# Attention beside an MLP on one core: the scale of Q from sums in PSUM, lengths once a chunk, V's read-outs first

## The chip, the cores and the metric

The kernel runs on one core of a Trainium2 chip. Its engines work side by side, each through its own instructions in order: TensorE (PE in the profile; PEld are its weight loads), VectorE (DVE), ScalarE (ACT), GpSimd (POOL) and SyncE (SP), which here only issues DMAs. The metric is the device time of one execution in microseconds; the three runs of the kernel before took 1353.08, 1352.74 and 1349.31 us, median 1352.74.

## What is computed

One input x of 2048 rows and 640 columns is normalized. The result is x plus an attention block of 32 heads (head size 20) plus an MLP block of width 1536, both on the normalized rows:

```python
def _A_ref(x, wqkv, wo):
    qkv = (x @ wqkv).reshape(B, S, 3, H, Dh).transpose(2, 0, 3, 1, 4)
    q, k, v = qkv[0], qkv[1], qkv[2]
    p = softmax(einsum("bhqd,bhkd->bhqk", q, k) * Dh ** -0.5)
    o = einsum("bhqk,bhkd->bhqd", p, v)
    return o.transpose(0, 2, 1, 3).reshape(B, S, D) @ wo
def _B_ref(x, w1, b1, w2, b2):
    y = layernorm(x)
    return gelu(y @ w1 + b1) @ w2 + b2
xn = layernorm(A_x)
return A_x + _A_ref(xn, A_wqkv, A_wo) + _B_ref(xn, B_w1, B_b1, B_w2, B_b2)
```

S = 2048, D = 640, H = 32, everything float32.

## The kernel before, in words

The kernel has a **head** (to about 218 us of the span), which makes Q, K and V and prepares the weights, and a long **loop** over head pairs, half sequences and key blocks, into which the MLP and the output projection are woven by credits. The change lies in the head alone, and the head's order is the order in which the program is written: each engine gets its instructions in that order and takes them strictly one after the other.

Float32 values are split into a high and a low float16 part, and a product is made of three float16 passes (`PASS`). So that the parts lie in range, each weight matrix gets a scale, a power of two from the sum of its squares. `squares` adds up along the free dimension on ACT (one accumulator column for each piece), `pow2` adds over partitions with a matmul against a 128x128 tile of ones (`L111`), adds the columns on DVE (`L112`) and makes a power of two from the exponent bits (`L113` to `L117`, `exponents` at `L99`); `scale_of` makes from it the scale (`L421`) and, for Q and K, the factor `qks` for the way back (`L424`), which the read-outs of Q and K use. `split_qkv` (`L429` on ACT, `L430` on DVE) makes the parts.

**The start.** The first 512 rows are normalized, transposed on PE (`L535`, against the identity `ident`; the fifth column block follows at `L539` into the one buffer of the PSUM pool `psM`, tag `m`), while ACT sums the squares of Q's weights. Behind the sixteen transposes of the first four blocks PE runs the sum for the scale of Q, then the copies `xnt` (`L543`, `L544`) and splits alternate with the first products.

**The chunks.** The rows go in four chunks `c` of 512. For each, five tile pairs `tt` (256 columns of Q or K) are made: `qk` (`L323`), its read-out `qk_out` (`L338` on ACT, `L339` on DVE, two stores to `qkscr` from SP), and the squares of what was read out, `qk_sq`, into a tile `sq` (even `tt`: pool `pa`, two buffers; odd `tt`: the tag `qs` of the pool `stp`, also two). `lengths` takes squares from the list `pend` and adds them head by head with small matmuls (`L368`, four for each block of 128 columns) in PSUM; it is called with four blocks at `tt == 3` and with the remaining six behind V's second tile (in the last chunk behind V's first). Then four tiles of V follow: `vproj` (`L396`) and `vproj_out` (`L406` on ACT; for half of the key blocks `L408` on DVE too).

**Other work between.** `some(n)` takes the next `n` steps of the weight work (`weights`): squares of w2 and w1, their scales, `factors`, which at `tt == 4` of chunk 1 squares b1 (`L95`) and sums it by `pow2` on PE, and the splits (`L126` to `L128`), among which the scale of wo is made in chunk 2. `norm_a`, `norm_b` and `norm_c` normalize the next chunk's rows; `norm_c` ends with a DMA from POOL that stores 512 row scales of 4 bytes each (`rscr`, `L272`). Chunk 1 is transposed on PE (`transp`, `transp_out`). Chunks 2 and 3 are transposed by DMA: `turn` writes a `row` tile (`L304` on ACT, `L305` on DVE; three buffers) and SP issues its transposition (`L306`). It is called behind `qk_out` for row 0 at `tt == 2`, rows 1 and 2 at `tt == 3`, row 3 at `tt == 4`; when row 3 has landed, SP stores the chunk (`L309`) for the MLP.

**Buffers.** A tile takes the buffer of its tag that came free first, and its first writer waits until the last user of that buffer has finished; for a `row` tile that is the DMA. The pool `psS` has three PSUM buffers, taken in turn by the products, V's tiles, the transposes and the sums of `pow2` other than Q's and K's.

Of the kernel before, what the change touches and what calls it, by code (L numbers as in the profile page):

```python
# [16 lines left out]
P = 128  # L17
# [25 lines left out]
def mha_mlp_kernel(tc, x, wqkv, wo, w1, b1, w2, b2, out):  # L43
# [4 lines left out]
    with (  # L48
# [53 lines left out]
        def pow2(acc, tag):  # L102

            lo = keep.tile([P, 1], F32, name=f"lo_{tag}")
            hi = keep.tile([P, 1], F32, name=f"hi_{tag}")
            if tag in ("q", "k"):
                pt = psM.tile([P, 512], F32, tag="m", name="mxp")
            else:
                pt = psS.tile([P, 2, 512], F32, tag="s", name="mxp")[:, 0, :]
            n = acc.shape[1]  # L110
            nc.tensor.matmul(pt[:, :n], ones, acc, start=True, stop=True)  # L111
            nc.vector.tensor_reduce(lo, pt[:, :n], AX.X, ALU.add)  # L112
            nc.vector.tensor_scalar(lo, lo, 2.0**-100, 2.0**120, ALU.max, ALU.min)  # L113

            nc.vector.tensor_scalar(lo.bitcast(I32), lo.bitcast(I32), 0x7F000000, 1,
                                    ALU.bitwise_and, ALU.logical_shift_right)
            nc.vector.tensor_scalar(lo, lo, 2.0**64, None, ALU.mult)  # L117
            exponents(lo, hi)
            return lo, hi

        pw = {}
# [40 lines left out]
        with tc.tile_pool(name="pa", bufs=2) as pa, tc.tile_pool(name="pa1", bufs=1) as pa1, tc.manual_schedule():  # L162
# [135 lines left out]
            def turn(c, j):  # L298

                if j == 0:  # L300
                    xnts[c] = pa.tile([P, KD, 2, 512], F16, tag="xnt", name=f"xnt{c}")
                xv = xts[c][j].rearrange("p (k n) -> p k n", k=KD)
                row = pa.tile([P, KD, 2, P], F16, tag="row", name="row", bufs=3)
                nc.scalar.activation(row[:, :, 0, :], xv, AF.Copy)  # L304
                nc.vector.tensor_sub(row[:, :, 1, :], xv, row[:, :, 0, :])  # L305
                nc.sync.dma_start(xnts[c].rearrange("p k s t -> p (k s) t")[:, :, j * P : (j + 1) * P],  # L306
                                  row.rearrange("p k s n -> p (k s n)"), transpose=True)
# [105 lines left out]
            accs, scales = {}, {}  # L413
# [4 lines left out]
            def scale_of(tag):  # L418
                pw[tag] = pow2(accs[tag], tag)
                scales[tag] = keep.tile([P, 1], F32, name=f"s_{tag}")  # L420
                nc.vector.tensor_scalar(scales[tag], pw[tag][1], 4096.0, None, ALU.mult)  # L421
                if tag in "qk":
                    q = "qk".index(tag)
                    nc.vector.tensor_scalar(qks[:, q : q + 1], pw[tag][0], QKTOP, 2.0**-22, ALU.min, ALU.mult)  # L424
# [107 lines left out]
            pt = [pts[0][:, 0], pts[0][:, 1], pts[1][:, 0], pts[1][:, 1]]  # L532
            for j in range(4):
                for k in range(KD - 1):
                    nc.tensor.transpose(pt[k][:, j * P : (j + 1) * P], xts[0][j][:, k * P : (k + 1) * P], ident)  # L535
            scale_of("q")
# [5 lines left out]
            for k in range(KD):  # L542
                nc.scalar.activation(xnts[0][:, k, 0, :], pt[k], AF.Copy)  # L543
# [6 lines left out]
            for c in range(4):  # L550
                nxt = c + 1 if c < 3 else None
                for tt in range(5):
# [11 lines left out]
                    if tt == 3:  # L564
                        lengths(4)
# [37 lines left out]
                for j in range(4):  # L603
                    ps = vproj(c, j)
                    if j == (0 if c == 3 else 1):
                        lengths(10)
                    if c == 0:
# [13 lines left out]
                    vproj_out(c, j, ps)  # L621
# [658 lines left out]
```

## Time and profile before

| | |
|---|---|
| runs | 1353.08, 1352.74, 1349.31 us; median 1352.74 |
| the profiled execution | 1349.61 us, of it span 1347.7 us; mean granted clock 0.999 |
| busy over the span | PE 1330.8 us (99%), ACT 1128.6 (84%), DVE 1055.8 (78%), POOL 37.9 (3%) |
| the head | to 218.51 us, where the loop's first matmul (`L709`) stands |
| HBM traffic | 82.14 MB read, 42.51 MB written |

How to read the lines that follow. A **timeline** row is: start in us, duration in us, engine, line of the kernel, operation, output<-inputs, shapes, count; in brackets the idle time of the engine before it and what ended it. Neighbouring instructions of one kind are merged into one row ("x4"), with the first start and the stretch to the last end. A **stage table** row is: the stretch, its length, then busy time and count of instructions for PE, PEld, DVE, ACT and POOL, then the granted PE clock (1.00 is full), the DMA share and GB/s. A **DMA issue** row gives the median time from issue to landing at its end. Matmuls are pipelined: the duration of one is longer than the distance to the next.

### The profile page before, as it was taken

The numbers are of one execution on the slowest core, as the hardware profiler recorded it, in microseconds if no ns is written. First come the engines' busy times: TensorE is split into PE (matmuls) and PEld (weight loads), VectorE is DVE, ScalarE is ACT, GpSimd is POOL, SyncE is SP. The second block draws the span as 40 slices with busy tenths as digits, with TensorE's granted clock in tenths as the row PEclk, the third lists the DMA queues.
The fourth block names the chain that finished last, engine by engine and source line by source line (L and its number), as shares of the span: only waits on it lengthen the run. The fifth ranks groups of instructions, "written<-read, shape, count | busy, mean of one in ns | idle before, by whom it ended". The sixth has DMA issues, their size and how long they took to land.

```text
span 1347.7 us, 29060 instructions
## 1 busy us (share of the span) xinstructions
PE 1330.8 (99%) x11647; PEld 590.7 (44%) x11647; DVE 1055.8 (78%) x1436; ACT 1128.6 (84%) x1306; POOL 37.9 (3%) x85
## 2 busy tenths in 40 slices
PE   9999999999999999999999999999999999999997
PEld 6645545443334333434343343434433333333475
DVE  6756935998779887978897789787878898888632
ACT  7754525999999999999999999999999999998700
POOL 3011000000000000000000000000000000000000
PEclk9999999999999999999999999999999999999999
DMA  8767732121112222222322141313032322244375
GB/s 277 246 201 183 145 107 58 34 62 34 48 60 70 86 83 63 53 58 77 105 61 61 29 111 48 91 52 94 19 87 63 95 66 83 70 139 125 103 223 178
DMA packets 100153, 129.58 MB, mean 96 GB/s; under 512 B 24276, under 2 KB 66328, under 8 KB 100012
## 3 DMA queue, kind: packets, MB, share of 16 engines
q1 hardware_dynamic: 96652, 120.25, 30.4%
q0 software_dynamic: 2912, 6.90, 2.9%
q8 instruction: 93, 1.52, 0.5%
q10 hardware_dynamic: 448, 0.51, 0.2%
q14 instruction: 48, 0.39, 0.1%
HBM read 82.14 MB, written 42.51 MB: 92 GB/s over the span
## 4 chain that ended last, share of the span: by engine, by line
PE 83%; DVE 8%; ACT 4%; issue 2%; DMA 1%; SPq 1%; DVEq 0%; POOL 0%; ACTq 0%; POOLq 0%
PE o L740 26%; PE s L709 16%; PE py L1002 11%; PE qkp L323 10%; PE pu L971 9%; PE z L1081 5%; PE vp L396 5%; DVE low L723 4%; ACT p L711 3%; PE warm L220 1%; DMA lt<-lpart 1%; DVE u L908 0%; ACT ev L761 0%; DVE u L918 0%; DVE u L910 0%
## 5 line engine op out<-in xcount | busy, mean ns | idle before, releaser
L711 ACT ACTIVATE p<-s 128x1024 f32<-128x1024 f32 x1024 | 971.4, 1042 | 41.2 <-PE s L709 35.4
L723 DVE TENSOR_TENSOR low<-p 128x1024 f16<-128x1024 f32 x512 | 614.6, 1219 | 155.6 <-ACT p L711 155.5
L740 PE MATMUL o<-p,vfull 128*32 128x512 bf16 (+1 forms) x4096 | 429.8, 493 | 0.0
L709 PE MATMUL s<-qs,ks 61*128 61x512 f16 x2048 | 315.8, 381 | 6.3 <-ACT p L711 5.5
L709 PEld LDWEIGHTS <-ks 61*128 61x128 f16 x2048 | 63.1, 94 | 291.5 <-issue 289.3
L1002 PE MATMUL py<-w2t,hT 128*128 128x320 f16 x1152 | 178.4, 300 | 1.7 <-DVE xb L936 0.9
L971 PE MATMUL pu<-xm,w1t 128*128 128x256 f16 x1440 | 179.3, 273 | 0.0
L971 PEld LDWEIGHTS <-w1t 128*128 128x128 f16 x1440 | 130.5, 98 | 67.4 <-issue 53.9
L1002 PEld LDWEIGHTS <-hT 128*128 128x128 f16 x1152 | 102.6, 98 | 89.6 <-issue 55.3
L323 PE MATMUL qkp<-xnt,wv 128*128 128x512 f16 x600 | 131.1, 379 | 0.4 <-ACT vfull L406 0.2
L740 PEld LDWEIGHTS <-vfull 128*32 128x32 f16 x3072 | 59.5, 95 | 133.6 <-issue 102.9
L740 PE MATMUL o<-low,vfull 128*32 128x512 f16 x1024 | 102.5, 378 | 0.4 <-DVE low L723 0.2
L323 PEld LDWEIGHTS <-wv 128*128 128x128 f16 x600 | 58.3, 98 | 70.0 <-DVE wv L430 1.1
L740 PEld LDWEIGHTS o<-p,vfull 128*32 128x32 f32 x2048 | 62.3, 108 | 53.2
L338 ACT ACTIVATE qkhl<-qkp,qks 128x1024 f16<-128x1024 f32 (+1 forms) x24 | 23.2, 966 | 55.1 <-PE qkp L323 34.4
L396 PE MATMUL vp<-wv,xnt 128*128 128x320 f16 x480 | 66.7, 299 | 0.0
L1081 PE MATMUL z<-w1t,ot 128*128 128x320 f16 x480 | 66.3, 299 | 0.0
L1081 PEld LDWEIGHTS <-ot 128*128 128x128 f16 x480 | 46.5, 98 | 20.8 <-issue 3.0
L396 PEld LDWEIGHTS <-xnt 128*128 128x128 f16 x480 | 46.7, 98 | 18.4
L339 DVE SCALAR_TENSOR_TENSOR qkhl<-qkp,qks,qkhl 128x1024 f16<-128x1024 f32 (+1 forms) x24 | 26.5, 1105 | 32.0 <-ACT qkhl L338 31.9
L1040 DVE SCALAR_TENSOR_TENSOR acc<-z,sc,acc 128x320 f32<-128x320 f32 x32 | 17.4, 547 | 42.8 <-PE z L1081 39.4
L992 POOL DMA_DIRECT2D xb<-in_B_b_dram x16 | 13.8, 863 | 1018.7 <-DMA xb<-in_A_x_dram 624.8
(188 smaller groups left out, 699.8 us busy)
## 6 DMA issues: line engine op xcount, KB each, us to landing
qkscr<-qkhl SPq DMA_DIRECT2D x40, 256.0 KB
opart<-ev SPq DMA_DIRECT2D x124, 80.0 KB
ks<-qkscr SPq DMA_DIRECT2D x120, 80.0 KB
qs<-qkscr SPq DMA_DIRECT2D x192, 40.0 KB
oa<-opart SPq DMA_DIRECT2D x32, 240.0 KB
xt<-in_A_x_dram SPq DMA_DIRECT2D x16, 320.0 KB
xscr<-xnt SPq DMA_DIRECT2D x4, 1280.0 KB
xm<-xscr SPq DMA_DIRECT2D x8, 640.0 KB
```

The costliest lines, as they stand in the source:

```text
L323: nc.tensor.matmul(ps[:, i, :], wv[:, k, q, a, mm * P : (mm + 1) * P], xnts[c][:, k, b, :], start=(k + n == 0), stop=(k == KD - 1 and n == 2))
L338: nc.scalar.activation(hl[:, 0, i0:i1], ps[:, i0:i1], AF.Copy, scale=a)
L339: nc.vector.scalar_tensor_tensor(hl[:, 1, i0:i1], ps[:, i0:i1], a, hl[:, 0, i0:i1], ALU.mult, ALU.subtract)
L396: nc.tensor.matmul(ps[:, hf, :320], xnts[c][:, k, a, j * P : (j + 1) * P], wv[:, k, 2, b, hf * 320 : (hf + 1) * 320], start=(n == 0), stop ...
L709: nc.tensor.matmul(ps[:, a, :], ks[64 * a : 64 * a + 61, kb * P : (kb + 1) * P], qs[64 * a : 64 * a + 61, cc * 512 : (cc + 1) * 512], star ...
L711: nc.scalar.activation(pt, ps, AF.Exp, scale=QS)
L723: nc.vector.tensor_sub(low, pt, upper(pt))
L740: nc.tensor.matmul(pv.o[32 * q : 32 * q + 32, :], src[:, v0 - PAD * (1 - q % 2) :][:, :32], t, start=q not in pv.begun, stop=last, skip_gr ...
L971: nc.tensor.matmul(ps[:, i], w1v[:, k, (f + i) // 4, a, fo_ : fo_ + P], xnt[:, k, b, :], start=(n == 0), stop=(n == 3 * KD - 1))
L1002: nc.tensor.matmul(ps[:, :320], hTs[mc][:, f, a, j * P : (j + 1) * P], w2v[:, f, b, hf * 320 : (hf + 1) * 320], start=(n == 0), stop=(n == ...
L1040: nc.vector.scalar_tensor_tensor(acc[:, cols], ps[:, :320], fo, acc[:, cols], ALU.mult, ALU.add)
L1081: nc.tensor.matmul(ps[:, :320], ot[:, k, a, j * P : (j + 1) * P], wov[:, k, b, h * 320 : (h + 1) * 320], start=(n == 0), stop=(n == 3 * KD ...
```

## The change

Five edits in the head.

1. The scale of Q. The five columns of Q's sums of squares are added over partitions *and* over columns by five one-column matmuls into one PSUM column `pq`, which stand between the sixteen transposes (two after the first row block's, one after the second's, one after the third's, and the last in the middle of the fourth's). DVE reads that column directly; for Q the factor 2^64 is folded into the constants, and what only the way back needs (`whole`, `qks`) runs in `back("q")` behind the loop of copies and splits.
2. `lengths(4)` at `tt == 3` runs only in chunk 3; in the other chunks all ten blocks are added behind V's second tile.
3. `sq` has three buffers in place of two.
4. `row` has two buffers in place of three.
5. In chunk 0, V's tiles 1 to 3 are read out directly behind their products, ahead of the normalizing, transposing and weight work.

```diff
-        def pow2(acc, tag):
+        def pow2(acc, tag, total=None):
...
-            n = acc.shape[1]
-            nc.tensor.matmul(pt[:, :n], ones, acc, start=True, stop=True)
-            nc.vector.tensor_reduce(lo, pt[:, :n], AX.X, ALU.add)
-            nc.vector.tensor_scalar(lo, lo, 2.0**-100, 2.0**120, ALU.max, ALU.min)
+            if total is None:
...
+                nc.tensor.matmul(pt[:, :n], ones, acc, start=True, stop=True)
+                nc.vector.tensor_reduce(lo, pt[:, :n], AX.X, ALU.add)
+                total = lo
+            nc.vector.tensor_scalar(lo, total, 2.0**-100, 2.0**120, ALU.max, ALU.min)
 
             nc.vector.tensor_scalar(lo.bitcast(I32), lo.bitcast(I32), 0x7F000000, 1,
                                     ALU.bitwise_and, ALU.logical_shift_right)
+            if tag == "q":
+                scales[tag] = keep.tile([P, 1], F32, name=f"s_{tag}")
+                nc.vector.tensor_scalar(hi.bitcast(I32), lo.bitcast(I32), 0x3F800000, None, ALU.bitwise_xor)
+                nc.vector.tensor_scalar(scales[tag], hi, 2.0**76, None, ALU.mult)
+                return lo, hi
+            whole(lo, hi)
+            return lo, hi
+
+        def whole(lo, hi):
             nc.vector.tensor_scalar(lo, lo, 2.0**64, None, ALU.mult)
             exponents(lo, hi)
...
-                row = pa.tile([P, KD, 2, P], F16, tag="row", name="row", bufs=3)
+                row = pa.tile([P, KD, 2, P], F16, tag="row", name="row", bufs=2)
...
-                    sq = pa.tile([P, 2, 512], BF16, tag="sq", name="sq", bufs=2)
+                    sq = pa.tile([P, 2, 512], BF16, tag="sq", name="sq", bufs=3)
...
+            def back(tag):
+                if tag == "q":
+                    whole(*pw[tag])
+                q = "qk".index(tag)
+                nc.vector.tensor_scalar(qks[:, q : q + 1], pw[tag][0], QKTOP, 2.0**-22, ALU.min, ALU.mult)
...
+            pq = psM.tile([P, 512], F32, tag="m", name="mxq")
             for j in range(4):
                 for k in range(KD - 1):
                     nc.tensor.transpose(pt[k][:, j * P : (j + 1) * P], xts[0][j][:, k * P : (k + 1) * P], ident)
-            scale_of("q")
+                    if (j, k) in ((0, 3), (1, 3), (2, 3), (3, 1)):
+                        for i in ((0, 1), (2,), (3,), (4,))[j]:
+                            nc.tensor.matmul(pq[:, :1], ones, accs["q"][:, i : i + 1], start=i == 0, stop=i == KD - 1)
+            scale_of("q", pq[:, :1])
...
                 split_qkv("q", [k], 0, 2 * P)
+            back("q")
...
-                    if tt == 3:
+                    if tt == 3 and c == 3:
                         lengths(4)
...
+                    if c == 0 and j > 0:
+                        vproj_out(c, j, ps)
                     if c == 0:
                         if j < 2:
                             (norm_b, norm_c)[j](1)
...
                     some(2 if c < 3 else 1)
-                    vproj_out(c, j, ps)
+                    if c > 0 or j == 0:
+                        vproj_out(c, j, ps)
```

More of the change, by code (lines that the diff above doesn't have):

```diff
@@ L412, in mha_mlp_kernel, with scale_of @@
             junk = pa1.tile([P, 3 * D], BF16, name="junk")
-            accs, scales = {}, {}
+            accs = {}
             def sums(tag, ws):
                 accs[tag] = squares(ws, junk)
[L418 to L424, printed above, removed]
+            def scale_of(tag, total=None):
+                pw[tag] = pow2(accs[tag], tag, total)
+                if tag not in scales:
+                    scales[tag] = keep.tile([P, 1], F32, name=f"s_{tag}")
+                    nc.vector.tensor_scalar(scales[tag], pw[tag][1], 4096.0, None, ALU.mult)
+                if tag == "k":
+                    back(tag)
+            def back(tag):
[3 more added lines that the diff above has]
+                nc.vector.tensor_scalar(qks[:, q : q + 1], pw[tag][0], QKTOP, 2.0**-22, ALU.min, ALU.mult)
             def split_qkv(n, ks=range(KD), c0=0, c1=D):
```

12 lines of the change are left out of this document (6 added, 6 removed).

## The prediction

> **What bounds the kernel now.** I read the page first, then the stage table (busy time of each engine by stretch), then the timeline of the head, then the waits and the DMA queues of single windows. Two rows of the stage table say what counts: TensorE (PE) is busy for the whole of every stretch, in the head and in the long loop.
>
> ```profile
> 102.00:119.00 17.00, 17.00 (x148) 12.14 (x147) 13.59 (x31) 8.73 (x13) 1.08 (x2) 1.00 1.00 225
> 225.00:1300.00 1075.00, 1066.59 (x9919) 433.15 (x9912) 899.74 (x1079) 1009.46 (x1130) 15.22 (x18) 1.00 0.26 73
> ```
>
> The second column is PE: 17.00 of 17.00 us in a stretch of the head, 1066.6 of 1075 in the loop, at a granted clock of 1.00. So the end of the kernel moves by whatever holds or frees PE in the head (0 to 218 us), one for one, and work on ACT, DVE or the queues costs nothing until PE runs into it. The change touches only the head. What it can win is the little that PE loses there; what it can lose is larger, since PE executes in order.
>
> **Part 1, the scale of Q.** The present chain, from the timeline:
>
> ```profile
> 12.10 2.04 PE L535 MATMUL pt<-ident,xt 128*128 128x128 f32 x16
> ...
> 13.95 0.60 ACT L543 ACTIVATE xnt<-pt 128x512 f16<-128x512 f32 x1 [0.40 <-PE pt L535]
> 13.97 0.28 PE L111 MATMUL mxp<-acc,ones 128*128 128x5 f32 x2
> 14.29 0.16 DVE L112 TENSOR_REDUCE lo_q<-mxp 128x1 f32<-128x5 f32 x1 [0.87 <-PE mxp L111]
> ...
> 15.24 0.15 DVE L421 TENSOR_SCALAR s_q<-hi_q 128x1 f32<-128x1 f32 x1
> ...
> 15.43 0.51 ACT L429 ACTIVATE wv<-w1t,s_q 128x256 f16<-128x256 f32 x1 [0.88 <-DVE s_q L421]
> ...
> 16.00 10.67 PE L323 MATMUL qkp<-xnt,wv 128*128 128x512 f16 x48 [0.16 <-ACT wv L429]
> ...
> 20.67 2.46 DVE L430 SCALAR_TENSOR_TENSOR wv<-w1t,s_q,wv 128x256 f16<-128x256 f32 x6
> ```
>
> From the reduction (14.29) to the last operation (15.24) are five steps of 0.19 us. The change leaves four operations, three steps: 0.38 us are gone. But PE now runs five one-column sums instead of one five-column sum, four of them before the one that counts. What one costs I read in chunk 1, where such a pair stands before V's matmuls:
>
> ```profile
> 101.94 0.28 PE L111 MATMUL mxp<-acc,ones 128*128 128x1 f32 x2
> 101.97 8.08 PEld L396 LDWEIGHTS <-xnt 128*128 128x128 f16 x60
> 102.08 8.31 PE L396 MATMUL vp<-wv,xnt 128*128 128x320 f16 x60
> ```
>
> 0.14 us from the pair to the next matmul. Four extra are 0.56 us; two transposes now stand behind the last sum (about 0.12 us each, 1.87 us over 16), which takes 0.23 off, and some is covered where PE waited for the normalized rows. The sum comes some 0.25 us later, the chain is 0.38 us shorter: a gain of about **0.1 us**, between a loss of 0.2 (nothing covered) and a gain of 0.4 (all covered). ACT's first copy (13.95) slips by the pairs too, but ACT idles 0.88 us behind it. The three DVE operations moved behind the loop cost 3 x 0.15 us at 20.67, ahead of the split of the next columns; PE asks for these columns only after 30 of the 48 matmuls, at 16.00 + 30/48 x 10.67 = 22.7, so they are hidden; with no cover they would cost 0.45 us.
>
> **Part 2, lengths once a chunk.** The small matmuls on the squares are moved, not removed.
>
> ```profile
> L368 PE MATMUL norms<-sq,heads 128*32 128x128 bf16 x96 | 2.3, 221 | 0.0
> ```
>
> 96 in 2.3 us is 0.38 us for a group of 16, so joining a group to another can win between 0 and 0.38 us; only the hand-over between kinds of matmul is saved, and I take **0.1 us** for each of chunks 0, 1 and 2.
>
> **Part 3, V's read-outs first (chunk 0).** One wait of PE goes:
>
> ```profile
> 68.16 0.69 ACT L406 ACTIVATE vfull<-vp 128x640 f32<-128x640 f32 x1
> 68.31 0.30 PEld L111 LDWEIGHTS mxp<-acc,ones 128*128 128x128 f32 x2
> 68.41 0.28 PE L111 MATMUL mxp<-acc,ones 128*128 128x6 f32 x2
> ...
> 68.90 6.42 PE L323 MATMUL qkp<-xnt,wv 128*128 128x512 f16 x29 [0.21 <-ACT vfull L406]
> ```
>
> The first tile of chunk 1 takes the PSUM buffer that the read-out at 68.16 frees. With that read-out some 5 us earlier PE goes on at 68.41 + 0.14 = 68.55: **0.35 us** won (from 0 to 0.49). The price is on DVE: one 0.8 us read-out ahead of the second Newton step, so POOL's store of the row scales goes out about 0.9 us later; nothing in the head reads it.
>
> **Part 4, the buffers.** The third buffer for squares is paid for with the third buffer of `row`, and here I expect the time to go. Four rows are transposed by DMA per chunk: row 0 after tile pair 2, rows 1 and 2 together after pair 3, row 3 after pair 4. With three buffers only row 3 has to wait for a transfer (row 0's). With two, ACT may write row 2 only when row 0's transposition has landed. Chunk 1:
>
> ```profile
> 80.57 0.89 DVE L241 BATCH_NORM_STATS2 st<-xt 128x6 f32<-128x320 f32 x2 [1.97 <-DMA xt<-in_A_x_dram]
> ...
> 94.07 1.48 SPq L306 DMA_TRANSPOSE xnt<-row  x1
> ...
> 94.55 0.79 POOL L272 DMA_DIRECT2D rscr<-r  x1 [3.41 <-DVE r L229]
> ...
> 96.06 1.35 ACT L304 ACTIVATE row<-xt 128x640 f16<-128x640 f32 x2
> ...
> 97.31 0.20 ACT L95 ACTIVATE junk<-b1t 128x12 bf16<-128x12 f32 x1
> 97.42 0.19 ACT L95 ACTIVATION_READ_ACCUMULATOR junk<-b1t 128x1 f32 x1
> ...
> 104.12 0.74 ACT L304 ACTIVATE row<-xt 128x640 f16<-128x640 f32 x1 [0.81 <-DMA xnt<-row]
> ```
>
> ```profile
> rscr<-r POOLq DMA_DIRECT2D x1, 2.0 KB, 9.1
> ```
>
> Row 3 (104.12) did wait, 0.81 us, and for row 0's landing: so row 0, issued at 94.07, landed at about 104.1, 10 us later. The store of the row scales, issued 0.5 us behind it, took 9.1 us from issue to landing (94.55 + 9.1 = 103.65): the two come out together. With two buffers row 2, now written from 96.06 + 0.62 = 96.68 (two in 1.35 us, 0.73 each), starts at 104.12: **7.4 us later, with ACT blocked.** Behind it on ACT stand the square of b1 (97.31), the first split of w2, and the read-out of pair 4. The square's accumulator is read until 97.61, then at 105.05; PE's one-column sum (101.94) needs it and stands in PE's order ahead of all of V's matmuls. PE goes on at 105.15 instead of 101.94: **+3.2 us.** The moment hangs on a landing, and that on x's landing (80.57: DVE waited for it), not on PE; so what parts 1 to 3 won by then, 0.1 + 0.1 + 0.35 + 0.1, about 0.65 us, only lengthens PE's wait. Were the landing to move with PE, they would come off.
>
> Row 3 then waits for row 1, and everything behind it slips by some 4 us. PE asks for the transposed chunk only after V's four tiles (two take 8.31 us, so 16.6 us in all) and is itself 3.2 us late, so this stays hidden, as do V's read-outs.
>
> Chunk 2 has the same pattern, with the store of the scales ahead of row 0:
>
> ```profile
> rscr<-r POOLq DMA_DIRECT2D x1, 2.0 KB, 10.7
> ```
>
> ```profile
> 148.04 1.36 SPq L306 DMA_TRANSPOSE xnt<-row  x1
> ...
> 148.61 1.35 ACT L304 ACTIVATE row<-xt 128x640 f16<-128x640 f32 x2
> ...
> 149.86 1.33 ACT L126 ACTIVATE wtmp<-w1t,s 128x512 f32<-128x512 f32 x2
> ...
> 151.82 1.55 DVE L305 TENSOR_TENSOR row<-xt,row 128x640 f16<-128x640 f32 x2
> 151.89 8.31 PE L396 MATMUL vp<-wv,xnt 128*128 128x320 f16 x60
> ...
> 154.35 0.15 DVE L112 TENSOR_REDUCE lo_o<-mxp 128x1 f32<-128x5 f32 x1
> ...
> 155.33 1.11 ACT L338 ACTIVATE qkhl<-qkp,qks 128x1024 f16<-128x1024 f32 x1 [4.14 <-DMA qkscr<-qkhl]
> ...
> 156.56 0.74 ACT L304 ACTIVATE row<-xt 128x640 f16<-128x640 f32 x1
> ```
>
> Row 3 (156.56) holds row 0's buffer, so row 0 has landed by 156.56; a store of q/k that SP had issued before it landed at 155.33, which I take as the other end. Row 2 goes from 149.23 to 156.56 (or 155.33). DVE's second half of the pair starts at 157.29 instead of 152.55, 4.74 us later, and the reduction for wo (154.35), behind one split on DVE, goes to 159.1. (That split reads what ACT writes behind row 2: 0.66 us, from 157.2, so it is there in time.) That reduction frees the PSUM buffer that V's second tile takes (buffers go out in the order in which they came free); V's second half would start at 151.89 + 4.15 = 156.04 and now starts at about 159.35: **+3.3 us** (2.1 with the early end), less 0.1 for part 2.
>
> Sum: +3.2 + 3.3 - 0.1 = **+6.4 us**. The profiled execution took 1349.61 us around its span of 1347.7, so it would take 1356.0. The median of the three runs, 1352.74, lies 3.1 us above it; the time asked for is a median, so I put the difference on that: 1359.1.
>
> **Rivals.**
>
> *The clock falls during the wait.* PE would stand still for 3.2 + 0.65 = 3.9 us in chunk 1 and 3.3 in chunk 2. At the end of the kernel PE stops too:
>
> ```profile
> 1340.00:1341.00 1.00, 0.89 (x7) 0.40 (x5) 0.07 (x1) 0.00 (x0) 0.00 (x0) 1.00 0.53 170
> ...
> 1344.00:1345.00 1.00, 0.00 (x0) 0.00 (x0) 0.00 (x0) 0.00 (x0) 0.00 (x0) 0.86 0.07 16
> 1345.00:1346.00 1.00, 0.00 (x0) 0.00 (x0) 0.00 (x0) 0.00 (x0) 0.00 (x0) 0.50 0.02 8
> ```
>
> The last matmul ends at 1340.89 and the clock halves at 1344.72 (0.86 of that microsecond), 3.8 us later; it then stays at 0.50 to the end, 3.0 us. So the chunk 1 wait sits right at the edge. 3 us at half clock cost 1.5 us: +7.9, or 1360.6; with both waits 1362.1. The Trainium skill (TensorE: Matmul & The Clock Gate, What's actually happening) says that PE drops to half rate after an idle window of about 3.4 us that runs free of the kernel, and comes back after a busy one. The trace agrees as far as 3.8 us goes; by that rule a fall would cost 1.7 us, an estimate from the page. 15%.
>
> *Row 0 of chunk 1 lands in time.* It was issued 0.5 us before the store that holds it up, so a small shift could let it through; then row 2 starts where it does now and chunk 1 costs nothing. Left: 3.2 (or 2.0) - 0.65: +1.4 to +2.6, so 1354.1 to 1355.3. Against it: both hang on the same run of DVE operations, whose order is not changed. 18%.
>
> *Not slower: the transpositions land early in both chunks.* The mechanism is the row-scale store: were it to hold the queues up for a shorter time than 9 to 11 us, row 0 would be there when it matters. In chunk 1 row 2 may start 3.7 us late (its accumulator at 97.61, PE's sum at 101.94 - 0.65) before PE feels it, so a landing up to 6.3 us after issue is free; in chunk 2 DVE's backlog (152.55 against 149.96) and the reduction's (154.51 against 156.04) give 4.1 us, so 5.3 us after issue. Beyond these points it costs what is over. Inside them only the gains remain: -0.75, 1352.0. Both stores measured here were slow; 7%.
>
> *Something in the loop gains from the later start* by over 0.3%: nothing in the loop reads the head's order; 3%, as for all that I don't see.
>
> **How the numbers follow.** The forecast has 57%, the others 15, 18, 7 and 3. A measurement of this kernel tells about 0.3%, 4.06 us, from no change. Slower by more: the forecast, but for the part of it (about 3) in which the early end of chunk 2 and unpinned gains come together, and the clock case: 0.69. Within: the second and third rivals and the rest of the forecast: 0.27. Faster: 0.04. The range runs from 1353.5, which takes in the second rival, to 1362.5, both waits at half clock; outside are the gain and the unseen.
>
> **What would show it.** In the timeline of the changed kernel: a wait of ACT at L304 (its new line number aside) for `xnt<-row` of about 7 us in both chunks, on the second of the two rows; PE idle about 3.9 us before V's first tile of chunk 1, released by ACT's square of b1, and about 3.3 us before V's second tile of chunk 2, released by DVE's reduction for wo; no wait of PE for V's read-out at the start of chunk 1; the first Q matmul near 15.9. I am wrong if ACT's wait is short, if PE is not held behind it, or if the loop starts within 2 us of 218.5.

## The result, and the profile after

The changed kernel is **slower: 1364.34 us against 1352.91 us** (medians of six runs each, taken together on one chip), ratio 1.0085, 95% interval 1.0071 to 1.0099. Two later comparisons (e9, e16 below) gave 1.0074 (1.0060 to 1.0088) and 1.0070 (1.0058 to 1.0082). Forecast were 1359.1 us, 6.4 above before; 11.4 came, above the range's end of 1362.5. Direction and place were right, the size was not.

The waits of the changed kernel, for PE and for ACT (total us, times, longest us). The lines of the chunks stand 11 further down in the code than before (`L304` is `L315`, `L396` is `L407`), those of `pow2`'s sum one (`L111` is `L112`):

```profile
PE mxp L112 <- ACT junk L95: 8.8, 1, 8.8
PE vp L407 <- DVE lo_o L113: 2.5, 1, 2.5
...
ACT row L315 <- DMA xnt<-row: 20.6, 3, 12.9
```

These are the two waits of PE that the forecast named, with the releasers that it named: ACT's square of b1 in chunk 1, DVE's reduction for wo in chunk 2. The first is 8.8 us in place of 3.9. The timeline of chunk 1 shows why:

```profile
96.52 1.48 SPq L317 DMA_TRANSPOSE xnt<-row  x1
...
97.00 0.79 POOL L283 DMA_DIRECT2D rscr<-r  x1 [3.41 <-DVE lo L115]
...
109.24 0.74 ACT L315 ACTIVATE row<-xt 128x640 f16<-128x640 f32 x1 [12.86 <-DMA xnt<-row]
...
109.99 0.19 ACT L95 ACTIVATION_READ_ACCUMULATOR junk<-b1t 128x1 f32 x1
...
110.23 0.58 PE L112 MATMUL mxp<-acc,ones 128*128 128x1 f32 x2 [8.82 <-ACT junk L95]
...
110.67 10.68 PE L407 MATMUL vp<-wv,xnt 128*128 128x320 f16 x60
```

Row 2 (109.24) waits for row 0's buffer. Row 0 was issued at 96.52, not at 94.07, and landed 12.6 us later, not 10. Behind ACT stand the accumulator (109.99), PE's sum and V: V starts at 110.67 in place of 102.08, 8.6 us late. And its first 60 matmuls take 10.68 us in place of 8.31. The stage table (stretch; its length; busy time and count of PE, PEld, DVE, ACT, POOL; granted clock; DMA share; GB/s) says why:

```profile
101.00:105.00 4.00, 0.41 (x2) 0.00 (x0) 0.00 (x0) 0.00 (x0) 0.00 (x0) 1.00 1.13 77
105.00:110.00 5.00, 0.00 (x0) 0.00 (x0) 0.00 (x0) 0.76 (x3) 0.00 (x0) 0.53 1.10 63
110.00:115.00 5.00, 4.77 (x19) 2.92 (x20) 4.57 (x22) 2.86 (x6) 0.00 (x0) 0.50 0.82 187
...
170.00:173.00 3.00, 3.00 (x14) 1.71 (x12) 2.93 (x7) 2.09 (x4) 0.00 (x0) 0.53 0.51 145
```

The granted clock (0.53, 0.50) is half from 105.3 to 115.5 us, five of these microseconds under V's matmuls, and once more around 170 to 173.5. That is behind chunk 2's wait:

```profile
162.63 4.23 PE L407 MATMUL vp<-wv,xnt 128*128 128x320 f16 x30
...
166.57 0.74 ACT L315 ACTIVATE row<-xt 128x640 f16<-128x640 f32 x1 [7.25 <-DMA xnt<-row]
...
169.15 0.15 DVE L113 TENSOR_REDUCE lo_o<-mxp 128x1 f32<-128x5 f32 x1
...
169.36 5.91 PE L407 MATMUL vp<-wv,xnt 128*128 128x320 f16 x30 [2.49 <-DVE lo_o L113]
```

ACT's wait (7.25) is the forecast's 7.3; PE loses 2.5 us where 3.3 were forecast, and 30 matmuls take 5.91 us where they took 4.23 a tile earlier. The loop's first matmul stands at 233.80 in place of 218.51. These rows sum to it: 8.6 + (10.68 - 8.31) + 2.5 + (5.91 - 4.23) = 15.1 of 15.3 us. The span grew by 15.9; this profiled execution took 1365.29 us, near the median after, while that of before, 1349.61, lies 3.3 us under its median.

What the other parts did, in the timeline of the start and of chunk 0's end:

```profile
11.92 0.60 PE L554 MATMUL pt<-ident,xt 128*128 128x128 f32 x4
...
14.52 0.16 DVE L115 TENSOR_SCALAR lo_q<-mxq 128x1 f32<-128x1 f32 x1 [1.80 <-PE mxq L558]
...
15.09 0.15 DVE L123 TENSOR_SCALAR s_q<-hi_q 128x1 f32<-128x1 f32 x1
...
15.90 8.41 PE L334 MATMUL qkp<-xnt,wv 128*128 128x512 f16 x38
...
60.07 0.79 POOL L283 DMA_DIRECT2D rscr<-r  x1 [3.94 <-DVE r L240]
...
68.36 0.28 PE L112 MATMUL mxp<-acc,ones 128*128 128x6 f32 x2
...
68.50 3.83 PE L334 MATMUL qkp<-xnt,wv 128*128 128x512 f16 x17
```

The chain on DVE is 0.57 us long, was 0.95; but from the first transpose to the first product of Q 3.98 us pass, before 3.90. PE's wait for V's read-out is gone: 0.14 us from the sum to the product, was 0.49. The store of chunk 1's row scales goes out at 60.07; before, it went out at 59.40. And DVE's wait for x, ahead of chunk 2's normalization, was 1.97 us with an end at 80.57; now:

```profile
83.03 0.89 DVE L252 BATCH_NORM_STATS2 st<-xt 128x6 f32<-128x320 f32 x2 [4.82 <-DMA xt<-in_A_x_dram]
```

2.46 us later, and row 0 is issued 2.45 us later.

### The profile page after: what moved, and what is told of

Read it like the earlier page. It is cut to its first block, busy times and chain, and to the rows that moved or that the text cites. A ratio compares the mean times of both kernels' runs of the same rounds, so it can differ in the third digit from the quotient of the medians.

```text
span 1363.6 us, 29082 instructions
## 1 busy us (share of the span) xinstructions
PE 1335.3 (98%) x11655; PEld 593.6 (44%) x11655; DVE 1056.0 (77%) x1436; ACT 1129.0 (83%) x1306; POOL 37.5 (3%) x85
## 4 chain that ended last, share of the span: by engine, by line
PE 76%; DVE 11%; ACT 5%; DMA 4%; issue 2%; SPq 1%; ACTq 0%; DVEq 0%; POOL 0%; POOLq 0%
PE o L767 26%; PE s L736 17%; PE py L1029 11%; PE pu L998 9%; PE z L1108 5%; DVE low L750 4%; PE vp L407 4%; ACT p L738 3%; PE qkp L334 3%; DMA xnt<-row 2%; DMA wos<-in_A_wo_dram 1%; DMA xt<-in_A_x_dram 1%; PE warm L231 1%; DVE qkhl L350 1%; DVE st L252 1%
## 5 line engine op out<-in xcount | busy, mean ns | idle before, releaser
L407 PE MATMUL vp<-wv,xnt 128*128 128x320 f16 x480 | 70.9, 310 | 2.5 <-DVE lo_o L113 2.5
L407 PEld LDWEIGHTS <-xnt 128*128 128x128 f16 x480 | 48.4, 102 | 23.5 <-issue 2.7
L788 ACT ACTIVATE ev<-o 128x512 f32<-128x512 f32 x64 | 39.4, 615 | 2.7 <-PE o L767 2.7
```

Source lines behind the costliest of these rows:

```text
L407: nc.tensor.matmul(ps[:, hf, :320], xnts[c][:, k, a, j * P : (j + 1) * P], wv[:, k, 2, b, hf * 320 : (hf + 1) * 320], start=(n == 0), stop ...
L788: nc.scalar.activation(evs[g, hf][:, cc], pv.o, AF.Copy)
```

## Experiments

Theory A: nearly all of the loss is the second `row` buffer, because the 4-byte store of the row scales holds up row 0's landing, and ACT now waits for that. Theory B: the later store of chunk 1's row scales (part 3) costs extra, since the transfers behind it, x's among them, land later. Theory C: a good part is PE's half clock, not the wait itself. Against A stood that ACT's wait could be covered; against B that DVE and the queues have room; against C that PE's wait alone could account for everything.

All ratios stand against the kernel before, run beside it on the same chip (its medians there: 1349.5 to 1349.8 us).

| run | what it is | median us | ratio, 95% interval |
|---|---|---|---|
| e1 | before + two `row` buffers | 1357.24 | 1.0062 (1.0045 to 1.0078) |
| e2 | scale and V's read-outs alone | 1354.07 | 1.0032 (1.0019 to 1.0045) |
| e3 | changed + 72 and 18 idle passes | 1360.37 | 1.0083 (1.0067 to 1.0100) |
| e4 | changed, store written later in the program | 1358.59 | 1.0071 (1.0054 to 1.0088) |
| e5 | scale alone | 1351.24 | 1.0010 (0.9996 to 1.0023) |
| e6 | V's read-outs alone | 1352.92 | 1.0020 (1.0010 to 1.0030) |
| e7 | V's read-outs behind the store | 1349.44 | 0.9997 (0.9984 to 1.0011) |
| e8 | changed, late stores inside the loop | 1347.91 | 0.9986 (0.9976 to 0.9995) |
| e9, e16 | changed, again | 1359.19, 1358.64 | 1.0074, 1.0070 (intervals above) |
| e10 | changed + 62 and 18 idle passes | 1360.17 | 1.0072 (1.0058 to 1.0086) |
| e11 | three `row` buffers, all late stores in the loop | 1348.92 | 0.9994 (0.9985 to 1.0003) |
| e12, e18 | before + buffers + lengths | 1357.73, 1360.13 | 1.0060 (1.0046 to 1.0073), 1.0084 (1.0070 to 1.0097) |
| e13 | changed, V's read-outs behind the store | 1358.79 | 1.0072 (1.0059 to 1.0085) |
| e14 | before, chunk 1's store later by itself | 1353.95 | 1.0022 (1.0012 to 1.0032) |
| e15 | changed, chunk 1's store in the loop | 1358.16 | 1.0066 (1.0054 to 1.0078) |
| e17 | e12 + 28 idle passes | 1358.44 | 1.0062 (1.0049 to 1.0074) |

The same kernel came out at 1357.73 and 1360.13 at two times (e12, e18). So a difference under some 2.5 us between kernels that weren't run side by side says nothing. Run side by side were e1 to e4, e5 to e8, e9 to e12, e13 to e16, and e17 with e18.

### The buffers alone (e1, e12, e18)

```diff
-                row = pa.tile([P, KD, 2, P], F16, tag="row", name="row", bufs=3)
+                row = pa.tile([P, KD, 2, P], F16, tag="row", name="row", bufs=2)
```

e12 and e18 have the third `sq` buffer and the joined lengths as well.

> The kernel before with one edit alone: the row tile has two buffers in place of three. Theory (the loss is the row buffer): ACT waits 7 to 13 us for row 0's transposition before row 2 of chunk 2 and some 7 us in chunk 3's rows, PE waits 3 to 9 us for the square of b1 and 2 to 3.5 us for the reduction for wo, the PE clock falls to half during the first wait; the time is 8 to 13 us above the kernel before, like the changed kernel. Rival (the order of V's read-outs or of the lengths makes the loss): within 2 us of the kernel before.

> The kernel before with part 2 and part 4 alone: two buffers of row, three of squares, lengths once a chunk. If my price for the lengths holds (0.1 us a chunk), this equals the run with two buffers of row alone: ratio 1.006, 1356.5 to 1358. If joining the groups moves work on PE's order so that something else comes late, it is 1 us or more above that; a gain of up to 1 us is possible if each group's 0.38 us goes.

> The same without the idle passes, for comparison on this chip: ratio 1.006 as before, the clock at half for 6.8 us from about 104.5 us.

e12's waits of PE and its timeline:

```profile
PE mxp L111 <- ACT junk L95: 3.9, 1, 3.9
PE vp L396 <- DVE lo_o L112: 1.6, 1, 1.6
```

```profile
94.12 1.48 SPq L306 DMA_TRANSPOSE xnt<-row  x1
...
104.60 0.74 ACT L304 ACTIVATE row<-xt 128x640 f16<-128x640 f32 x1 [7.74 <-DMA xnt<-row]
...
106.03 11.02 PE L396 MATMUL vp<-wv,xnt 128*128 128x320 f16 x60
```

Here row 0 is issued as before (94.12) and ACT waits 7.74 us; 7.4 were forecast. V starts 3.95 us late, its first tiles take 2.71 us longer at half clock, and chunk 2 adds 1.65: 8.3 us of the 8.5 by which the loop starts late. Two buffers and lengths give 1.0060 and 1.0084, the whole change 1.0070 to 1.0085: **the buffers are the loss**, and no part of it is left that these runs can tell. e1 without the lengths (1.0062; 7.7 us, just under the 8 to 13 expected) agrees with the forecast that joining them is worth next to nothing. e18 missed its 1.006: row 0 was issued at 95.32 and held until 106.3, though V's edit isn't in it.

### The store that holds the landing (e4, e8, e11)

```diff
-                nc.gpsimd.dma_start(rscr[c * 512 : (c + 1) * 512].rearrange("(j p) -> p j", p=P), r2)
+                if c >= 2:
+                    late.append((c, r2))
...
+                    if (g, hf, cc, kb0) == groups[3]:
+                        for c, r2 in late:
+                            nc.vector.tensor_scalar(r2, r2, 1.0, None, ALU.mult)
+                            nc.gpsimd.dma_start(rscr[c * 512 : (c + 1) * 512].rearrange("(j p) -> p j", p=P), r2)
```

That is e8; e4 lacks the multiplication by 1.0. e11 moves the stores from chunk 1 on, in a kernel with parts 1 and 3 only (three `row` buffers, lengths as before).

> The changed kernel with two row buffers, but the stores of the row scales of the last two chunks are issued in the loop (third group) instead of in the head. Theory (the store of 512 values of 4 bytes holds back row 0's landing): row 0 lands 3 us after its issue in both chunks, ACT waits under 1 us for row 2, PE does not wait, the clock stays at 1.00, and the time is within 2 us of the kernel before, 0.5 to 1 us below it if anything. Rival (the transpositions or the loads of wo are slow by themselves): row 0 still lands 8 us or more after its issue and the time stays 7 us or more above the kernel before.

> The changed kernel, with a DVE operation on the row scales of the last two chunks (times 1.0) in the loop's fourth group and their store behind it, so that POOL can't issue it in the head. Theory (the 4-byte store holds back row 0's landing): row 0 lands 3 to 4 us after its issue in both chunks, ACT waits under 1.5 us for row 2, PE does not wait for the square of b1 nor for the reduction for wo, the clock stays at 1.00, and the time is within 2 us of the kernel before. Rival (the loads of wo or the transpositions are slow by themselves): row 0 lands 8 us or more after its issue, and the time stays 7 us or more above.

> Scale and V's read-outs changed, three buffers of row, two of squares, lengths as before, and the stores of the row scales of chunks 1 to 3 moved into the loop. If the 2 KB store is what holds up the landings, rows land 3 to 5 us after issue in chunk 1 and 2, PE has no wait over 0.5 us in the head, and the time is 1346 to 1348.5, at or below the run with two buffers and late stores (1347.9). If the store isn't the cause, the result is that of scale and V's read-outs alone, about 1354.

e4 didn't test what it was made for. POOL had nothing to wait for and issued the store in the head all the same, where the scales were ready; its timeline has it under the loop's line:

```profile
96.00 0.79 POOL L1166 DMA_DIRECT2D rscr<-sc  x1 [3.41 <-DVE lo L115]
```

In e8 the store stands behind a DVE operation of the loop. Its timeline and stage table:

```profile
95.04 1.52 SPq L321 DMA_TRANSPOSE xnt<-row  x1
...
98.79 0.74 ACT L319 ACTIVATE row<-xt 128x640 f16<-128x640 f32 x1 [2.81 <-DMA xnt<-row]
```

```profile
101.00:105.00 4.00, 4.00 (x32) 2.89 (x30) 3.69 (x17) 2.34 (x3) 0.00 (x0) 1.00 0.83 201
```

Row 0 lands 3.7 us after its issue (98.79 - 95.04) in place of 10 to 12.6, with the same two buffers and a later issue than before. ACT waits 2.8 us (under 1.5 was expected), PE not at all (4.00 of 4.00 us at clock 1.00).

One rival is left in chunk 1: POOL's load of `wos`, which stood behind the store, goes out at 92.06 in e8, ahead of row 0, and lands at 96.2, 1.1 us behind row 0's issue. Chunk 2 has no such load, and there e8 shows the same:

```profile
146.04 1.36 SPq L321 DMA_TRANSPOSE xnt<-row  x1
...
149.10 0.74 ACT L319 ACTIVATE row<-xt 128x640 f16<-128x640 f32 x1 [1.76 <-DMA xnt<-row]
```

3.1 us from issue to landing, where the changed kernel, with the store in the head, has 8.5 (158.03 to 166.57). So theory A is shown: take the store of 2 KB away, and the two buffers cost nothing. e4, which differs from e8 in little but that its store stays in the head, is the control (1.0071). e8 is **faster than both kernels**, 1.6 us under before (by its interval, a gain of 0.05 to 0.24%) and some 11 under the changed one, which was not run beside it. e11 equals before (1348.92; 1346 to 1348.5 was expected).

### The later store (e2, e5, e6, e7, e14; e13, e15)

V's order as in e7 and e13:

```diff
                     if c == 0:
-                        if j < 2:
-                            (norm_b, norm_c)[j](1)
+                        if j == 1:
+                            norm_c(1)
+                        if j > 0:
+                            vproj_out(c, j, ps)
+                        if j == 0:
+                            norm_b(1)
```

and the kernel before with the store alone later (e14):

```diff
                 newton(r2, ve, "b")
+                if c == 1:
+                    for _ in range(6):
+                        nc.vector.tensor_scalar(r2, r2, 1.0, None, ALU.mult)
```

> The changed kernel with row at three buffers, sq at two, and lengths at tile pair 3 of every chunk again: what is left of the change is the scale of Q and V's read-outs. Theory: no wait of PE above 0.5 us in the head, no wait of ACT for row 0 above 2 us, time within 2 us of the kernel before (gain 0.3 to 0.6 us, not to be told from no change). Rival: 5 us or more slower.

> The kernel before with the new chain to the scale of Q alone. Theory (the chain is a wash: four extra pairs of matmuls against two DVE steps): the first Q matmul within 0.2 us of the kernel before when counted from the first transpose, no new wait behind it, time within 1.5 us of the kernel before. Rival (it is this edit that makes the scale-and-V kernel 4.5 us slower): 3 to 5 us slower.

> The kernel before with V's read-outs of chunk 0 ahead of the other work, alone. Theory (the read-out on DVE delays the second Newton step, so the store of chunk 1's row scales and with it x's load and row 0's transposition of the next chunk come later, and what has slack of a few us before runs out of it): the store is issued 0.7 us later against V's second tile, row 0 of chunk 2's rows lands 1 us or more later, ACT waits 3 us or more for row 3, PE waits 2 to 4 us for a V read-out at the start of chunk 2; 3 to 5 us slower than before. Rival (V's read-outs only win): 0 to 0.5 us faster, no wait of PE above 0.5 us.

> As the V read-outs alone, but the second Newton step and the store of chunk 1's row scales stay ahead of V's read-out. Theory (it is the delayed store): the store goes out when it did before, row 0 lands as before, no wait of PE above 0.5 us, within 1.5 us of the kernel before. Rival (it is something else in the moved read-outs): as slow as the V read-outs alone.

> The kernel before, with six small DVE operations (multiplications of the row scales by 1.0, 0.19 us apart) ahead of the store of chunk 1's row scales: nothing but a store 1.1 us later. If the later store by itself is the price of V's read-outs, most runs come out 3 to 4 us above the kernel before (median ratio about 1.0025), as with V's read-outs alone. If it was another part of that edit, the ratio stays within 1.000 to 1.001, since DVE has room for 1.1 us there.

> The changed kernel, with the store of chunk 1's row scales issued ahead of V's second read-out again. If the later store is what the changed kernel loses beyond the two buffers of row, this comes to the run with buffers and lengths alone (ratio 1.006), 1.5 to 4 us below the changed kernel on the same chip. If the store's 1 us is no matter, it equals the changed kernel within 1 us.

> The changed kernel, with the store of chunk 1's row scales alone moved into the loop; the stores of chunks 2 and 3 stay. If the chain store, x's load, normalization, row 0's issue is right, DVE's wait for x is 0 to 2 us in place of 4.4 to 4.8, row 0 is issued before 94 us, and still lands about 10 us later beside chunk 2's store: ACT's wait stays at 7 to 8 us, and the time is that of the buffers alone, ratio 1.005 to 1.0065. If chunk 1's store had no part in it, the ratio stays at 1.0075 to 1.0085.

e2 was a surprise: the two parts that were to gain half a microsecond together cost 4.5. e5 and e6 split it up. The runs of these kernels lie either near 1349.5 us or some 3 to 5 us above. Of the runs beside e5 to e8, before had three of 31 above 1351.2, V's read-outs alone (e6) nine of ten, the scale alone (e5) five of ten, and V's read-outs with the store ahead (e7) two of ten. Nothing but a store 1.1 us later (e14) put seven of nine above 1351.2, where before had one of 14. The store, DVE's wait for x and what PE then waits for, in e14's timeline and waits:

```profile
60.51 0.79 POOL L275 DMA_DIRECT2D rscr<-r  x1 [3.89 <-DVE r L274]
...
82.04 0.89 DVE L241 BATCH_NORM_STATS2 st<-xt 128x6 f32<-128x320 f32 x2 [3.55 <-DMA xt<-in_A_x_dram]
...
110.61 0.74 ACT L307 ACTIVATE row<-xt 128x640 f16<-128x640 f32 x1 [7.42 <-DMA xnt<-row]
```

```profile
PE qkp L326 <- DVE vfull L411: 2.1, 1, 2.1
...
PE vp L399 <- DVE vfull L411: 0.9, 1, 0.9
```

DVE loses nothing by the six operations (its next one starts at 60.12, before at 60.20). But x is there 1.5 us later than in the profile of before (82.04 against 80.57), and row 3 (110.61), with all three buffers, waits 7.4 us for row 0 where it waited 0.8. V's read-outs stand behind it on ACT, and PE waits 3 us for them. So theory B holds **for the kernel before**: it stands on an edge, and a store 1 us later pushes it over. In the profiles of e2, e5 and e6 the clock was half for 3.41 us besides, behind PE's wait.

Where the edge lies, a comparison of all the profiles suggests; no run was made for it. SP's issue of x's load in the profile of before, and the store's time to its landing (last column):

```profile
69.71 2.86 SPq L179 DMA_DIRECT2D xt<-in_A_x_dram  x4
```

```profile
rscr<-r POOLq DMA_DIRECT2D x1, 2.0 KB, 10.2
```

The store, issued at 59.40, landed at 69.6, 0.1 us ahead of x's load. In the four profiles in which it had landed by then (before, e1, e7, e12) x was there 10.7 to 11.4 us after its load's issue; in the fourteen in which it hadn't, 11.4 to 13.4 us; in the two without that store in the head (e11, e15), 10.0 and 10.1. So a store under way seems to hold x's load as it holds row 0. It would explain e5 too, whose store goes out no later than before's (59.20) but took 10.8 us, past the issue of x's load at 69.48: x was there 12.5 us behind that issue.

For the changed kernel B found no support: with the store early again (e13) it took 1358.79, unchanged (e16, beside it) 1358.64; the expected 1.5 to 4 us didn't come. e15, with that store out of the head, is the clearest trace:

```profile
79.35 0.89 DVE L253 BATCH_NORM_STATS2 st<-xt 128x6 f32<-128x320 f32 x2 [1.49 <-DMA xt<-in_A_x_dram]
...
93.22 1.48 SPq L321 DMA_TRANSPOSE xnt<-row  x1
...
103.79 0.74 ACT L319 ACTIVATE row<-xt 128x640 f16<-128x640 f32 x1 [7.75 <-DMA xnt<-row]
...
163.16 5.61 PE L411 MATMUL vp<-wv,xnt 128*128 128x320 f16 x30 [2.78 <-DVE lo_o L113]
```

x lands early, row 0 is issued 1.6 us ahead of e16's (94.78) and is held 10.6 us all the same, by chunk 2's own store; PE reaches chunk 2's wait earlier and waits longer there (2.78; 1.4 in e16), and the clock falls behind it once more (30 matmuls in 5.61 us; 4.24 in e16). So what V's earlier start had won (105.22 against 107.10) is given back, and the loop starts no earlier (227.30 against 227.16). In the medians 0.5 us is left, less than the runs can tell.

### The clock (e3, e10, e17; e9, e16 and e18 beside them)

Idle passes that compute nothing used, inside PE's waits (72 or 62 in chunk 1, 18 in chunk 2; in e17, 28 in chunk 1 alone):

```diff
+                    if c == 1 and tt == 4:
+                        warm(14)
```

> The changed kernel with PE kept busy in its two waits: 36 pairs of matmuls on ones (0.22 us each, 8.0 us) ahead of the sum of b1's squares in chunk 1 and 9 (2.0 us) behind V's first tile in chunk 2, into a PSUM tile that nobody reads. Theory (part of the loss is the clock): the waits end at the same moments, the clock stays at 1.00, the matmuls behind the waits take 4.1 us per V tile instead of 5.3 to 5.9, and the time is 3 to 4.5 us below the changed kernel's. Rival (the clock costs nothing): the same time as the changed kernel or up to 2 us more.

> The changed kernel with idle matmuls that fill most of the two waits and end before them: 62 passes instead of 72 in chunk 1, where the earlier run of this kind ended about 0.9 us too late, 18 in chunk 2. They compute nothing that is used. If the half clock costs what the traces read (2.4 us on V's first half in chunk 1, 1.8 in chunk 2), this is 2.5 to 4.5 us faster than the changed kernel, and the granted clock stays at 1.00 from 105 to 175 us. If the waits alone are the cost and the clock adds nothing, it equals the changed kernel within 1 us.

> The changed kernel itself, beside the two runs below on the same chip. By my theory (row buffer with a held landing +7.7 us, the later store +4 us): 1361 to 1365 against 1349.5. If the +11.4 us of the first comparison belonged to that chip, it comes out near 1357, where the row buffer alone was.

> The changed kernel again, to stand beside the three others on one chip: ratio 1.007 to 1.0085.

> Two buffers of row, three of squares, lengths once a chunk, and 28 idle passes (about 3.2 us, they compute nothing that is used) inside the 3.9 us wait of chunk 1, so that they end before it does. If the half clock costs what V's four half-clocked microseconds read (60 matmuls in 11.0 us in place of 8.3), this is 2 to 2.7 us faster than the same kernel without them, ratio 1.004, with the granted clock at 1.00 from 100 to 115 us. If the two come out within 0.7 us, the time of the half clock is given back elsewhere or filled matmuls cost what they save.

In all three the granted clock stayed at 1.00 through both waits. e9 and e16 came out at or under the low end of what was expected, so the first comparison's 11.4 us is the upper end: 9.4 and 8.9 here. In the changed kernel no time came back: 1360.17 with the passes (e10), 1359.19 without (e9, beside it); in e10's profile row 0 was held for 11.5 us, in e9's for 10.1, and why stays open. e3 had its passes end 0.9 us after the accumulator was ready, and had no changed kernel beside it. e17 has a steadier partner, e18; the timelines of the two, e17 first:

```profile
100.61 3.29 PE L220 MATMUL warm<-ones 128*128 128x128 f32 x28
105.40 0.38 PE L111 MATMUL mxp<-acc,ones 128*128 128x1 f32 x2 [1.50 <-ACT junk L95]
105.65 8.31 PE L396 MATMUL vp<-wv,xnt 128*128 128x320 f16 x60
...
162.50 4.24 PE L396 MATMUL vp<-wv,xnt 128*128 128x320 f16 x30 [3.03 <-DVE lo_o L112]
```

```profile
107.27 0.59 PE L111 MATMUL mxp<-acc,ones 128*128 128x1 f32 x2 [5.48 <-ACT junk L95]
107.72 10.82 PE L396 MATMUL vp<-wv,xnt 128*128 128x320 f16 x60
...
165.79 4.24 PE L396 MATMUL vp<-wv,xnt 128*128 128x320 f16 x30 [1.73 <-DVE lo_o L112]
```

V's first tiles are 2.5 us shorter at full clock, and 1.3 of it goes again in chunk 2, where PE, now earlier, waits 3.03 us in place of 1.73 for the same reduction. The medians differ by 1.7 us (1358.44, 1360.13); 2 to 2.7 were expected. (The rest of the loop's 3.3 us earlier start in e17's profile is an earlier landing of row 0, 104.42 against 106.29; its head was 1.2 us ahead from the first transpose on.) Theory C holds in part: the half clock is real and costs time in the stretch, but what its cure brings at the end is between nothing (e10) and some 2 us (e17). How much of the changed kernel's 9.4 to 11.4 us it is stays open.

## Why the prediction was right and wrong

- **What bounds the kernel, and where the change lands:** right. No engine got more to do (PE's busy time rose from 1330.8 to 1335.3 us, 4.05 of it in the rows at half clock above); PE lost in the head, in front of the two instructions named, by the releasers named. ACT's waits were forecast at 7.4 and 7.3 us and measured at 12.86 and 7.25 in the changed kernel, 7.74 and 6.80 in e12.
- **Part 1:** forecast a gain of 0.1 us between -0.2 and 0.4; measured -0.08 (3.98 against 3.90 us). The chain got 0.38 us shorter, as worked out; the added sums took back all of it.
- **Part 2:** forecast 0.1 us a chunk. The rows agree: 16 and 24 small matmuls took 0.34 and 0.45 us to what follows them (before, 94.89 to 95.23 and 110.32 to 110.77), the 40 together 0.67 (e12, 116.99 to 117.66). The times of e1 and e12 can't show so little.
- **Part 3:** PE's wait went, 0.35 us, as forecast. Its price was put at nothing: "POOL's store of the row scales goes out about 0.9 us later; nothing in the head reads it". It went out 0.7 us later, and nothing reads it; but what lands behind it is read. In the kernel before, a later store alone costs most runs 4 us (e14). In the changed kernel its share couldn't be told from none (e13), so this error isn't shown to be what put the time beyond the range.
- **Part 4, chunk 1: the step that failed.** The mechanism was right, the term of +3.2 us was mis-sized twice; in the changed kernel's first profile it measured 8.6 us of wait and 2.4 of half clock, 11.0 of the 15.3 us by which the loop starts late. First, it took row 0's landing for a fixed time, 104.12. It moved from 103.8 (e15) to 109.2 (the changed kernel) with x's landing and with a hold of 10 to 12.6 us, and V's start with it: +3.95 us in e12, +8.6 in the changed kernel's first profile. The text named x's landing as what sets the moment, and then didn't ask what sets x's landing. Second, it priced the wait at full clock, and V's first 60 matmuls took 9.6 to 11.0 us in place of 8.31 (e9, e12, e15, e16, e18 and the first profile). Why the landing was as late as 109.2 in that one profile, and 105.5 and 105.7 in e9 and e16, stays open.
- **Part 4, chunk 2:** +3.3 us was forecast; 1.4 to 3.0 us were measured. PE goes on 2.8 us after the start of row 2 (166.57 to 169.36 in the changed kernel, 159.72 to 162.50 in e17), so it waits the less, the later it has finished V's first tile. The half clock behind this wait (1.7 us in the first profile) was left out here too.
- **The rivals.** *The clock falls during the wait* had 15% and came true in every profile with two buffers, the store in the head and nothing in the wait (the changed kernel three times, e1, e4, e12, e13, e15, e18), and in e2, e5 and e6 with three buffers. The "3.8 us" at the kernel's end were taken for an edge, from a single instance: in e1 the clock halved 2.5 us after the last matmul. The Trainium skill (TensorE: Matmul & The Clock Gate, What's actually happening) speaks of an idle window of about 3.4 us that runs free of the kernel. The trace agrees on the length and on free running: every half-clocked stretch of the head lasts 3.41 us or two or three times that, and in the changed kernel the second starts 16 such windows after the end of the first. It differs on idle: the clock fell after windows in which PE stood for 2.5 us only (the changed kernel, chunk 2), in e6 for 2.08; the last section has the rows. *Row 0 lands in time* and *not slower* failed, as ACT's 12.9 us show; e8 shows what the last rival asked for, landings 3.7 and 3.1 us after issue, and there the change does gain.
- **The range** ended at the clock case of the same landing time. It held no case of a later landing, though the rows of before showed a landing that hung on two transfers.

For the kernel of e12 the forecast's own terms, at their measured sizes, are 3.95 + 1.65 us of waits (6.5 were forecast) and 2.71 of half clock (none). For the changed kernel the later landing comes on top. The absolute forecast also put 3.1 us on the profiled time to reach the median; e9, where before had 1349.79, gave 1359.19. That distance looks like the edge again: four of the six runs of before in the first comparison lie at 1352.74 to 1355.31, the other two at 1349.31 and 1350.38, and the profile is of the lower kind. There is no profile of the upper kind, so this isn't shown.

## What to carry to other kernels

A small store that nothing reads still has a price: ask which transfers are in flight beside and behind it, and who waits for their landing. Before giving up a buffer that a DMA frees, take the longest time from issue to landing that the trace shows, and ask what sets the issue, for that may move too: here the landing moved by 5.1 us in one profile (104.12 to 109.24). And price a wait of PE of more than some 2 us with a stretch at half clock behind it.

## What the runs showed of the hardware

The store of 512 row scales of 4 bytes took 9.1 to 12.8 us from issue to landing in the head wherever the profile has its landing, and 8.8 us in the loop (e8), while 320 KB of wo's weights took 4.1 us without it beside them (e8) and these with it (the changed kernel's DMA issues, median us from issue to landing in the last column):

```profile
wos<-in_A_wo_dram POOLq DMA_DIRECT2D x1, 320.0 KB, 12.8
...
rscr<-r POOLq DMA_DIRECT2D x1, 2.0 KB, 12.0
```

The Trainium skill (DMA: Bandwidth & Descriptors, Rules for kernel authors) says that a last dimension that isn't contiguous becomes one descriptor for each element, and to rearrange it; this store is of that kind, and the runs add that its neighbours' landings are held with it. Why the hold is 10 us in some executions, 12.6 in the changed kernel's first and 15.0 in e14's stays open.

The clock goes by windows of 3.41 us. Counted in such steps from the falls, it was half in the head after every window at full clock in which PE stood for 2.08 us (e6) or more, and after none in which it stood for 1.93 us (e9, 161.21 to 164.62) or less. e6's stage table; PE stood for 3.41 us less its busy time, the number behind the comma:

```profile
118.08:121.49 3.41, 1.33 (x8) 0.56 (x7) 2.67 (x5) 1.84 (x3) 0.00 (x0) 1.00 0.98 268
121.49:124.90 3.41, 3.41 (x10) 1.21 (x8) 0.79 (x2) 1.67 (x4) 0.54 (x1) 0.50 1.03 400
```

e17's wait of 3.03 us in chunk 2 left the clock up: counted back from that profile's fall at 1349.18, a window ends at 161.34, inside the wait, which leaves 1.87 us to the one side and 1.16 to the other. At half clock, it stayed there after a window with 0.83 us of standing (e12) and came back after one with 0.58 (e15).

The clock also fell once where PE was busy with small work. In e10's stage table PE worked for 2.51 of 3.41 us, on 64-wide matmuls mostly, and the clock was half for the next 3.41 us, inside the loop:

```profile
1292.49:1295.90 3.41, 2.51 (x33) 2.47 (x34) 1.10 (x3) 0.00 (x0) 0.00 (x0) 1.00 0.92 264
1295.90:1299.31 3.41, 3.41 (x14) 1.97 (x14) 0.96 (x2) 0.00 (x0) 0.00 (x0) 0.50 0.42 154
```
